# Gate and up projections with tokens standing and weight columns moving, in 29 groups of a two-layer kernel

## The chip, the cores and the metric

The kernel runs on one core of one Trainium2 chip. The metric is device time in microseconds of one execution; the number for a kernel is the median of several runs. A profiled execution, taken separately, gives the trace that all durations below come from.

## What is computed

Two layers of two blocks each, on x of 2048 tokens by 512 features in bf16, with the same weights in both layers:

```
x = x + A(layernorm(x), k, v, shift_k, ssm_k, ssm_D)
x = x + B(layernorm(x), w_gate, w_up, w_down)
(both once more)

A: kv = v * (k shifted over 4 taps with shift_k)
   y  = causal convolution of kv with ssm_k along the 2048 tokens, by FFT, + kv * ssm_D
   return layernorm(x) * y
B: return (silu(z @ w_gate) * (z @ w_up)) @ w_down      # w_gate, w_up: 512 x 1792; w_down: 1792 x 512
```

The convolution does not depend on x: k, v and the two filters are the same in both layers.

## The kernel before

The 2048 tokens are cut into four blocks c = 0..3 of 512, and each block into two halves h of two rows of 128 tokens (row o = 0, 1). A unit is (layer, c, h): 256 tokens in one layer; there are 16 units and they run in the order of c, then layer, then h. The convolution is done by matmuls with cosine and sine tables (tiles fwd and inv; X, G, H, Z are spectra), block against block, and its matrix products lie between those of the units, as do its elementwise products on DVE.

For a unit, `prologue` normalises the two rows, multiplies by y, adds, normalises again and writes z (128 tokens x 512 features) for each row. A transposing DMA from SP's queue turns z into zT, whose layout is [128 features, 4 feature blocks kd, row o, 128 tokens]. Only unit (0, 0, 0), the first, turns z on PE, and there ACT copies row 0 and DVE row 1 out of PSUM (lines 940 and 938).

`ffn(unit)` then walks the 14 blocks ft of 128 hidden columns in groups of 4, 4, 4 and 2. For each group `gate_up` makes gate and up, and `down` accumulates the group's share of the output in two PSUM tiles pd, one for each row. Six blocks (SHARE) are done for two units at once, with 512 moving columns. In `gate_up` the weights stand (128x128) and the 256 tokens of zT move, so the result comes out with hidden columns on partitions, which is the side on which `down` needs it as its standing operand:

```
mm(ps.t[:, q * m * W:(q + 1) * m * W],
   [(wt[which].t[:, kd, ft * P:(ft + 1) * P], moving(kd)) for kd in range(KD)])
```

Two blocks ft share one PSUM tile pf of 512 columns. ACT takes gate out of PSUM through silu into sg (line 974) and copies up into ht (line 977); DVE multiplies ht by sg (line 979). `down` (line 994) reads ht standing and w_down moving, 512 columns. Line 323 is the helper `mm` through which gate, up and most of the convolution go. At the end ACT copies pd (line 1075) and DVE adds it to x (line 1078).

All instructions are first recorded as operations with an engine, a cost, their readers and writers (class Plan). The order in which they are issued on every engine is a table, ORDER, written out in the file; `Plan.order` only places buffers in the slots of their rings along that order, and semaphores do the rest at run time. Each engine works its queue in this order. SP's queue holds all loads, stores and transposing DMAs. Rings have a number of slots each, among them n 2, sg 2, ht 5 (also for temporaries t1 and t2), dn 1, pf 4 (PSUM) and zT 3.

Of the kernel before, what the change touches and what calls it, by code (L numbers as in the profile page):

```python
# [53 lines left out]
SHARE = {(1, 0, 1): 2, (0, 2, 0): 2, (1, 3, 0): 2}  # L54
ORDER = [
# [59 lines left out]
NZ = 3  # L115
# [127 lines left out]
def kernel(  # L243
# [705 lines left out]
    def gate_up(us, fts, k):  # L949
        m, n = len(us), len(fts)  # L950
        per = 2 // m
        sg = new("sg", "sg", [P, n, m, W], parts=n // per)
        ht = new("ht", "ht", [P, n, m, W], parts=n // per)
        zs = [zts[u] for u in us]

# [385 lines left out]
```

## Time and profile before

| | |
|---|---|
| Median of 3 runs | 343.09 us (342.76 to 343.57) |
| Profiled execution | 342.9 us, of which the span of the trace 341.1 us |
| PE busy | 336.9 us, 2563 matmuls; clock granted 1.00 |
| DVE, ACT, POOL busy | 282.4, 252.5, 37.3 us |
| Matmuls of gate and up | 1696 with 256 columns, 48 with 512 |
| Matmuls of down | 434 with 512 columns, 28 in the last unit with 320 or 192 |
| Transposing DMAs of SBUF data | 30 of z, 16 of the convolution |
| q8, instruction fetches | 20 packets of 16 KB |

A busy time is the union of the instructions' spans on that engine. Matmuls are pipelined: the mean duration of one is longer than the distance from one to the next, and their ends are modelled. PEld is the weight load, which runs beside matmuls. In a group's line the number after x is the count, then come busy us and mean ns, then the idle time of the engine just before these instructions and what ended it. The chain of waits goes back from the last instruction, at each step to what released it, or to the instruction before it on its engine; its columns are start, length, engine, tile and line.

### The profile page before, as it was taken

To read this page: it belongs to the slowest core of one execution; us is meant where nothing else is said; L and a number is where in the kernel's file an instruction comes from. 1 tells how busy PE (TensorE), PEld (TensorE's weight loads), DVE (VectorE), ACT (ScalarE), POOL (GpSimd) and SP (SyncE) were. 2 spreads that over 40 slices of the span, in tenths; PEclk is the share of its full clock that TensorE was granted. 3 is DMA by queue.
4 is the path that set the end of the run, shared out by engine and by line. 5 is a ranking of instruction groups with operands and counts; after the bars stand their busy time and mean duration, and the time that the engine had idled before them with its cause. 6 is when DMAs were issued, how large, how long until landed. Compare 5 with 4: busy or idle time off the path is not lost.

```text
span 341.1 us, 6468 instructions
## 1 busy us (share of the span) xinstructions
PE 336.9 (99%) x2563; PEld 242.8 (71%) x2563; DVE 282.4 (83%) x478; ACT 252.5 (74%) x496; POOL 37.3 (11%) x46
## 2 busy tenths in 40 slices
PE   8999999999999999999999999999999999999996
PEld 7657858678687567768587756768685877777683
DVE  8899999999999999999999999889997533726022
ACT  7899999999977475778999973768665545545451
POOL 4000100002106100103100100101101000001000
PEclk9999999999999999999999999999999999999999
DMA  7999314050224175010110224010101110001111
GB/s 280 333 320 341 52 31 63 0 156 1 34 46 94 31 102 164 3 30 2 33 20 13 48 46 125 0 33 1 33 0 44 36 33 0 17 16 21 27 33 31
DMA packets 42088, 22.95 MB, mean 67 GB/s; under 512 B 33989, under 2 KB 39882, under 8 KB 42058
## 3 DMA queue, kind: packets, MB, share of 16 engines
q1 hardware_dynamic: 41904, 22.49, 26.0%
q8 instruction: 20, 0.33, 0.4%
q14 instruction: 10, 0.08, 0.1%
q10 hardware_dynamic: 154, 0.05, 0.1%
HBM read 12.33 MB, written 2.10 MB: 42 GB/s over the span
## 4 chain that ended last, share of the span: by engine, by line
PE 94%; ACT 3%; DMA 1%; SPq 0%; issue 0%; ACTq 0%
PE pf L323 57%; PE pd L994 28%; PE ps L323 6%; PE ps L470 2%; DMA kn<-in_A_k_dram 1%; ACT H L431 1%; ACT Yk L729 1%; ACT ks L526 0%; ACT n L874 0%; PE pt L378 0%; PE pt L489 0%; ACT zT L940 0%; ACT X L431 0%; SPq L354 0%; ACT xc L1052 0%
## 5 line engine op out<-in xcount | busy, mean ns | idle before, releaser
L323 PE MATMUL pf<-zT,wg_sb 128*128 128x256 bf16 (+1 forms) x872 | 110.3, 276 | 0.0
L323 PE MATMUL pf<-zT,wu_sb 128*128 128x256 bf16 (+1 forms) x872 | 110.0, 275 | 0.1
L994 PE MATMUL pd<-wd_sb,ht 128*128 128x512 bf16 (+1 forms) x462 | 106.2, 373 | 0.0
L323 PEld LDWEIGHTS <-wu_sb 128*128 128x128 bf16 x872 | 85.3, 98 | 18.9 <-issue 0.6
L323 PEld LDWEIGHTS <-wg_sb 128*128 128x128 bf16 x872 | 85.3, 98 | 17.3
L977 ACT CAST ht<-pf 128x512 bf16<-128x512 f32 x112 | 65.0, 592 | 23.0 <-PE pf L323 22.8
L974 ACT ACTIVATE sg<-pf 128x512 bf16<-128x512 f32 x112 | 66.6, 606 | 20.8 <-PE pf L323 17.3
L994 PEld LDWEIGHTS <-ht 128*128 128x128 bf16 x462 | 45.0, 98 | 44.1
L979 DVE TENSOR_TENSOR ht<-ht,sg 128x1024 bf16<-128x1024 bf16 (+1 forms) x61 | 38.9, 642 | 19.8 <-ACT ht L977 13.7
L826 POOL TENSOR_TENSOR rstd<-ve,nhalf 128x2 f32<-128x2 f32 x24 | 25.1, 1047 | 192.6 <-DVE ve L824 192.6
L821 DVE BATCH_NORM_STATS2 bnst<-xc 128x6 f32<-128x512 bf16 x48 | 31.8, 684 | 0.5
L1075 ACT CAST dn<-pd 128x512 bf16<-128x512 f32 x30 | 17.2, 590 | 17.5 <-PE pd L994 17.5
L431 ACT ACTIVATE X<-ps 128x512 bf16<-128x512 f32 x32 | 18.9, 606 | 10.5 <-PE ps L323 10.0
L1078 DVE TENSOR_TENSOR xc<-xc,dn 128x1024 bf16<-128x1024 bf16 x15 | 10.3, 687 | 16.8 <-ACT dn L1075 16.8
L669 DVE TENSOR_TENSOR t<-X,G 128x2048 bf16<-128x2048 bf16 x18 | 21.9, 1218 | 0.1
L665 DVE TENSOR_TENSOR t<-X,G 128x2048 bf16<-128x2048 bf16 x18 | 21.9, 1219 | 0.0
L855 POOL TENSOR_TENSOR rstd<-ve,nhalf 128x2 f32<-128x2 f32 x8 | 8.4, 1052 | 78.5 <-ACT ve L853 78.5
L679 DVE TENSOR_TENSOR Z<-Z,t 128x2048 bf16<-128x2048 bf16 x12 | 14.7, 1221 | 0.3
L677 DVE TENSOR_TENSOR t<-t,t 128x2048 bf16<-128x2048 bf16 x12 | 14.6, 1220 | 0.2
L431 ACT ACTIVATE H<-ps 128x512 bf16<-128x512 f32 x24 | 14.2, 612 | 0.0
L901 DVE TENSOR_TENSOR n<-n,Yk 128x1024 bf16<-128x1024 bf16 x15 | 10.3, 690 | 3.1 <-ACT n L874 1.9
L323 PE MATMUL ps<-hs,fwd 128*128 128x512 bf16 x40 | 12.7, 379 | 0.1
(103 smaller groups left out, 321.8 us busy)
## 6 DMA issues: line engine op xcount, KB each, us to landing
hn<-in_A_ssm_k_dram SPq DMA_DIRECT2D x4, 512.0 KB, 5.5
vt<-in_A_v_dram SPq DMA_DIRECT2D x4, 512.0 KB, 5.6
xc<-in_A_q_dram SPq DMA_DIRECT2D x4, 512.0 KB, 4.9
out_dram<-xc SPq DMA_DIRECT2D x15, 128.0 KB, 1.8
wg_sb<-in_B_w_gate_dram SPq DMA_DIRECT2D x1, 1792.0 KB
wu_sb<-in_B_w_up_dram SPq DMA_DIRECT2D x1, 1792.0 KB, 8.0
wd_sb<-in_B_w_down_dram SPq DMA_DIRECT2D x1, 1280.0 KB, 11.6
kn<-in_A_k_dram SPq DMA_DIRECT2D x1, 512.0 KB, 4.3
```

The source lines that it names most:

```text
L323: nc.tensor.matmul(o, lhsT=lhsT, rhs=rhs, start=(n == 0), stop=(n == len(terms) - 1))
L431: add("ACT", act(D), lambda: nc.scalar.activation(out=view(), in_=ps.t[:], func=ACT.Copy, scale=scale), r=[ps], w=[(buf, keys)], conv=conv)
L665: dve(n * D, lambda t1=t1, part=part: nc.vector.tensor_mul(out=t1.t[:], in0=x.t[:, sl, 0, :], in1=g.t[:, sl, part, :]), [(x, key(slots, (0 ...
L669: dve(n * D, lambda t2=t2, part=part: nc.vector.tensor_mul(out=t2.t[:], in0=x.t[:, sl, 1, :], in1=g.t[:, sl, 1 - part, :]), [(x, key(slots ...
L679: dve(n * D, lambda t1=t1, part=part: nc.vector.tensor_add(out=z.t[:, sl, part, :], in0=z.t[:, sl, part, :], in1=t1.t[:]), [t1], [zk], con ...
L821: add("DVE", 0.6, lambda st=st, i=i: nc.vector.bn_stats(out=st.t[:], in_=xs[c].t[:, i, :]), r=[(xs[c], (i,))], w=[st])
L826: add("POOL", pw, lambda: nc.gpsimd.tensor_tensor(out=rstd.t[:], in0=ve.t[:], in1=nhalf.t[:].to_broadcast((P, n)), op=ALU.pow), r=[ve, nha ...
L974: add("ACT", act(D), lambda ps=ps, sl=sl: nc.scalar.activation(out=sg.t[:, sl], in_=ps.t[:], func=ACT.Silu), r=[ps], w=[(sg, (b,))], due=( ...
L977: add("ACT", act(D), lambda ps=ps, sl=sl: nc.scalar.copy(out=ht.t[:, sl], in_=ps.t[:]), r=[ps], w=[(ht, (b,))], due=(us[0], at, 1.5, "a"))
L979: dve(n * m * W, lambda: nc.vector.tensor_mul(out=ht.t[:], in0=ht.t[:], in1=sg.t[:]), [sg], [ht], due=(us[0], (k + n) / NF, 0.0, "h"))
L994: nc.tensor.matmul((pds[o] if not cs.start else pds[HP]).t[:, cs], lhsT=ht.t[:, q, at, o * P:(o + 1) * P], rhs=wt["d"].t[:, ft, cs], start ...
L1075: add("ACT", act(D), lambda o=o: nc.scalar.copy(out=dn.t[:, o, :], in_=pds[o].t[:]), r=[pds[o]], w=[(dn, (o,))], due=(unit, 1.0, 3.0, "h"))
```

## The change

In 13 of the 16 units the first two or three groups of four blocks ft (WIDE) are made by a new function, with operands exchanged: 128 tokens of zT stand and 512 columns of the weights move. That gives the result with tokens on partitions, one PSUM tile per row o. The product of gate and up is therefore turned by two transposing DMAs on SP's queue into the layout that `down` reads; `down` for row o waits for the part of row o only.

```
+WIDE = {(1, 3, 1): 3, (0, 3, 1): 2, (0, 3, 0): 3, (1, 2, 0): 2, (0, 2, 1): 2, (1, 1, 0): 3, (0, 1, 0): 2, (1, 0, 0): 2, (0, 0, 0): 2, (1, 2, 1): 2, (1, 1, 1): 2, (0, 1, 1): 2, (0, 0, 1): 2}
 ORDER = [
...
-    plan = Plan({"h": 1, ... "t4": 2, "n": 2, "jk": 1, "dn": 1, "ks": 2, "z": 3, "zT": NZ,
-                 "sg": 2, "ht": 5, "st": 8, ...
+    plan = Plan({"h": 1, ... "t4": 2, "jk": 1, "ks": 2, "z": 3, "zT": NZ,
+                 "w2": 10, "st": 8, ...
...
+    def gate_up_wide(unit, fts, k):
+        zT, f0 = zts[unit], fts[0] * P
+        sg = new("w2", "sg", [P, HP, D], parts=HP)
+        hn_ = new("w2", "hw", [P, HP, D], parts=HP)
+        ht = new("w2", "ht", [P, KD, 1, W], parts=HP)
+        for o in range(HP):
+            for which in ("g", "u"):
+                ps = new("pf", "pf", [P, D], F32)
+                def go(ps=ps, o=o, which=which):
+                    mm(ps.t[:], [(zT.t[:, kd, o, :], wt[which].t[:, kd, f0:f0 + D]) for kd in range(KD)])
+                add("PE", pe(KD, D), go, r=[(zT, (o,)), wt[which]], w=[ps], ...)
+                if which == "g":
+                    add("ACT", act(D), lambda ps=ps, o=o: nc.scalar.activation(out=sg.t[:, o], in_=ps.t[:], func=ACT.Silu), ...)
+                else:
+                    add("ACT", act(D), lambda ps=ps, o=o: nc.scalar.copy(out=hn_.t[:, o], in_=ps.t[:]), ...)
+        dve(HP * D, lambda: nc.vector.tensor_mul(out=hn_.t[:], in0=hn_.t[:], in1=sg.t[:]), [sg], [hn_], ...)
+        for o in range(HP):
+            add("SP", 1.25, lambda o=o: nc.sync.dma_start_transpose(
+                out=ht.t[:, :, 0, o * P:(o + 1) * P], in_=hn_.t[:, o].rearrange("p (k f) -> p k f", k=KD)),
+                r=[(hn_, (o,))], w=[(ht, (o,))], lat=1.5)
+        return ht
...
-        groups = left + [(None, rest[a:min(a + 4, cut)], (unit,)) for a in range(0, cut, 4)] \
+        groups = left + [(None, rest[a:min(a + 4, cut)], (unit,) if a // 4 >= WIDE.get(unit, 0) else None) for a in range(0, cut, 4)] \
...
-                ht = gate_up(us, fts, k)
+                ht = gate_up(us, fts, k) if us else gate_up_wide(unit, fts, k)
```

The rings n, sg, ht and dn become one ring w2 of ten slots of the same size, used also by the new tile hw. The table ORDER is another one throughout, with entries for the new operations: what follows what on every engine is new, not only around the new groups. A third way to start the first spectrum is added that is not selected. The numbers of operations on ACT, DVE and POOL and their sizes stay; PE has 2097 matmuls instead of 2563 (464 fewer in the groups, 2 fewer that only keep PE busy at the start), and SP has 58 more transposing DMAs of 128 x 512 each.

More of the change, by code (lines that the diff above doesn't have):

```diff
@@ L289, in span @@
         return slice(rows[0], rows[-1] + 1, rows[1] - rows[0])
-    plan = Plan({"h": 1, "k": 1, "v": 1, "hs": 1, "x": 2, "y": 2, "s8": 10, "t4": 2, "n": 2, "jk": 1, "dn": 1, "ks": 2, "z": 3, "zT": NZ,
-                 "sg": 2, "ht": 5, "st": 8, "mv": 6, "ve": 6, "rs": 6, "pf": 4, "pc": 2, "pd": 2, **RINGS})
+    plan = Plan({"h": 1, "k": 1, "v": 1, "hs": 1, "x": 2, "y": 2, "s8": 10, "t4": 2, "jk": 1, "ks": 2, "z": 3, "zT": NZ,
+                 "w2": 10, "st": 8, "mv": 6, "ve": 6, "rs": 6, "pf": 4, "pc": 2, "pd": 2, **RINGS})
     def new(ring, name, shape, dtype=BF16, parts=1):
@@ L651, in product @@
             sl = slots[0]
-            t1, t2 = new("ht", "t1", [P, 2, D]), new("ht", "t2", [P, 2, D])
+            t1, t2 = new("w2", "t1", [P, 2, D]), new("w2", "t2", [P, 2, D])
             for t, part in ((t1, 0), (t2, 1)):
@@ L746, in pair_product @@
     def pair_product(a, b, dst, slot, ks):
-        t1, t2 = new("ht", "t1", [P, 2, D]), new("ht", "t2", [P, 2, D])
+        t1, t2 = new("w2", "t1", [P, 2, D]), new("w2", "t2", [P, 2, D])
         for t, part in ((t1, 0), (t2, 1)):
@@ L888, in apply_norm @@
         nmr = shift_of(st, HP, due) if on_act or N_ACT(layer, c, h) else None
-        n = new("n", "n", [P, HP, D], parts=HP)
+        n = new("w2", "n", [P, HP, D], parts=HP)
         for o, i in enumerate(rows):
@@ L951, in gate_up @@
         per = 2 // m
-        sg = new("sg", "sg", [P, n, m, W], parts=n // per)
-        ht = new("ht", "ht", [P, n, m, W], parts=n // per)
+        sg = new("w2", "sg", [P, n, m, W], parts=n // per)
+        ht = new("w2", "ht", [P, n, m, W], parts=n // per)
         zs = [zts[u] for u in us]
@@ L980, in gate_up @@
         return ht
+    def gate_up_wide(unit, fts, k):
+        zT, f0 = zts[unit], fts[0] * P
+        assert list(fts) == list(range(fts[0], fts[0] + KD))
+        sg = new("w2", "sg", [P, HP, D], parts=HP)
+        hn_ = new("w2", "hw", [P, HP, D], parts=HP)
+        ht = new("w2", "ht", [P, KD, 1, W], parts=HP)
+        for o in range(HP):
+            at = (k + 2 * o) / NF
+            for which in ("g", "u"):
+                ps = new("pf", "pf", [P, D], F32)
+                def go(ps=ps, o=o, which=which):
+                    mm(ps.t[:], [(zT.t[:, kd, o, :], wt[which].t[:, kd, f0:f0 + D]) for kd in range(KD)])
+                add("PE", pe(KD, D), go, r=[(zT, (o,)), wt[which]], w=[ps], due=(unit, at + (which == "u") / 21, 0.0, None))
+                if which == "g":
+                    add("ACT", act(D), lambda ps=ps, o=o: nc.scalar.activation(out=sg.t[:, o], in_=ps.t[:], func=ACT.Silu),
+                        r=[ps], w=[(sg, (o,))], due=(unit, at, 1.0, "a"))
+                else:
+                    add("ACT", act(D), lambda ps=ps, o=o: nc.scalar.copy(out=hn_.t[:, o], in_=ps.t[:]),
+                        r=[ps], w=[(hn_, (o,))], due=(unit, at, 1.5, "a"))
+        dve(HP * D, lambda: nc.vector.tensor_mul(out=hn_.t[:], in0=hn_.t[:], in1=sg.t[:]), [sg], [hn_], due=(unit, (k + KD) / NF, 0.0, "h"))
+        for o in range(HP):
[3 more added lines that the diff above has]
+        return ht
     def down(unit, pds, ht, fts, us, k, first, end, own):
@@ L990, in go @@
                 def go(o=o, css=css):
-                    at = sorted(zts[u].slot for u in us).index(zts[unit].slot)
+                    at = sorted(zts[u].slot for u in us).index(zts[unit].slot) if us else 0
                     for cs in css:
@@ L998, in down @@
                 add("PE", pe(n) if not last else pe(n, css[0].stop - css[0].start), go,
-                    r=[ht, (wt["d"], sorted({int(ft >= GROUPS[0]) for ft in fts}))],
+                    r=[(ht, (o,)) if us is None else ht, (wt["d"], sorted({int(ft >= GROUPS[0]) for ft in fts}))],
                     w=[pds[o]] if not split else [pds[o], pds[HP]] if not last else [pds[HP if css[0].start else o]],
@@ L1030, in ffn @@
             if ht is None:
-                ht = gate_up(us, fts, k)
-                if len(us) > 1:
+                ht = gate_up(us, fts, k) if us else gate_up_wide(unit, fts, k)
+                if us and len(us) > 1:
                     shared.setdefault(nxt, []).append((ht, fts, us))
@@ L1072, in ffn @@
             rows = rows_of(h)
-            dn = new("dn", "dn", [P, HP, D], parts=HP)
+            dn = new("w2", "dn", [P, HP, D], parts=HP)
             for o in range(HP):
@@ L1100 @@
     h0 = load_h(0, "ACT", -70) if HQ == "ACT" else None
-    tapR = new("dn", "tapR", [KD, P, KS])
+    tapR = new("w2", "tapR", [KD, P, KS])
     def load_taps(after=()):
@@ L1229 @@
             butterfly(evx, X[0], 0, False)
+        elif X0 == "mix":
+            evx = spectrum("evx")
+            X[0] = spectrum("X0")
+            direct(vt[0], X[0], "pf", eng(XVE[:4]), (0, 2))
         else:
@@ L1235 @@
             butterfly(ev, G[0], 1, False)
-        if X0 == "half":
+        if X0 in ("half", "mix"):
             half(vt[0], evx, "bd", 1.0, "pf", eng(XVE[4:]), False)
```

117 rows, old and new, of the table ORDER are left out of this document.

## The prediction

> **What bounds the kernel now.** I read the page first, then the chain of waits in order of time, then the timelines of PE, ACT and DVE around 32 us, the groups by form, the windows, and last the transfers' landing times.
>
> ```profile
> PE 336.9 (99%) x2563; PEld 242.8 (71%) x2563; DVE 282.4 (83%) x478; ACT 252.5 (74%) x496; POOL 37.3 (11%) x46
> ```
>
> ```profile
> 31.57 0.62 ACT zT L940
> 32.23 1.91 PE pf L323 x16
> ...
> 284.99 10.48 PE pf L323 x96
> 295.47 6.04 PE pd L994 x28
> ...
> 332.49 5.66 PE pd L994 x38
> 338.17 0.32 ACT xc L1052
> ```
>
> From 32.23 to 338.17 us the chain holds nothing but PE. The view of waits gives PE two in all, 0.8 and 0.2 us, both before 6 us. The chain also gives what a matmul costs when others follow it: 10.48 us / 96 = 109.17 ns with 256 moving columns, 6.04 / 28 = 215.71 ns with 512. The means in the groups (273 and 379 ns) are latencies and overlap, so I don't use them.
>
> ```profile
> 31.28 0.42 DVE L938 COPY zT<-ptz 128x512 bf16<-128x512 bf16 x1
> 31.57 0.62 ACT L940 COPY zT<-ptz 128x512 bf16<-128x512 bf16 x1
> 32.23 1.91 PE L323 MATMUL pf<-zT,wu_sb 128*128 128x256 bf16 x16
> ```
>
> The first gate/up matmul waits for both halves of the first zT: DVE's copy is done at 31.70, ACT's at 32.19.
>
> ```profile
> L974 ACT ACTIVATE sg<-pf 128x512 bf16<-128x512 f32 x112 | 66.6, 606 | 20.8 <-PE pf L323 17.3 <-DVE ht L979 2.8
> L977 ACT CAST ht<-pf 128x512 bf16<-128x512 f32 x112 | 65.0, 592 | 23.0 <-PE pf L323 22.8
> L979 DVE TENSOR_TENSOR ht<-ht,sg 128x1024 bf16<-128x1024 bf16 x51 | 34.8, 685 | 19.3 <-ACT ht L977 13.5 <-ACT sg L974 5.7
> ```
>
> ```profile
> 30.00:60.00 30.00, 29.82 (x243) 22.74 (x241) 29.83 (x44) 29.71 (x66) 3.21 (x4) 1.00 0.43 84
> 60.00:90.00 30.00, 30.00 (x216) 20.94 (x215) 29.56 (x55) 29.65 (x60) 3.81 (x5) 1.00 0.22 54
> ...
> 270.00:300.00 30.00, 30.00 (x226) 21.95 (x225) 12.61 (x26) 14.95 (x28) 1.38 (x2) 1.00 0.12 27
> ```
>
> Columns: window, length, then busy time of PE, PEld, DVE, ACT, POOL, granted clock, DMA share, GB/s. Until 90 us all three engines are full; from 270 on DVE and ACT are half idle. The clock is 1.00 throughout.
>
> ```profile
> L908 SPq DMA_TRANSPOSE zT<-z x30: 1189/1210/2272, 47.6 to 314.1; - x30
> ...
> DMA to landing us min/median/max: 2.4/2.5/4.2
> ```
>
> This is the row for the transfer that the change adds: one 128x512 transpose holds SP's queue for 1.2 us and lands 2.4 to 4.2 us after its issue.
>
> **Part 1, matmuls.** The WIDE values add up to 29 groups. Such a group had 32 matmuls of 256 columns (4 column blocks x 4 terms x gate and up) and gets 16 of 512: the same 8192 columns, 16 instructions fewer. 32 x 109.17 = 3.493 us against 16 x 215.71 = 3.451 us. Over 29 groups: 464 x (2 x 109.17 - 215.71) = 464 x 2.63 ns = **1.22 us less**, all of it on the chain. The 512-column price also holds with a gate/up tile as output: the shared groups of before run eight of them from 201.38 to 203.11 us in PE's timeline, 216 ns each. The weight loads (98 ns each, 464 fewer, 45 us of PEld) lie beside matmuls and give nothing. A rule of the Trainium skill (Perfetto Trace Analysis, Identifying the Most-Contended Engine) would have me judge PE's headroom by LDWEIGHTS busy time and not by matmul busy time: by it PE has 29% of the span free and the 45 us would look like a prize. The spacing of 109 and 216 ns speaks against that here.
>
> **Part 2, the start.** In the new order PE's first 8 wide matmuls read only the second half of zT, the one DVE copies; only the ninth waits for ACT. So the start can move from 32.23 to DVE's 31.70 plus a hop, about 31.75: 0.48 us. ACT's zT copy now stands behind a squared-sum pass (0.62 us with its read) and an X eviction (0.48): 31.57 + 1.10 + 0.62 = 33.29, needed at 31.75 + 8 x 0.2157 = 33.48. Covered, with 0.2 to spare; if that cover fails, the loss is the same order as the gain. Against it: ACT does one H eviction more (0.48) ahead of the first Yk, on which the chain to zT hangs. Bounds: 0.5 gained to 0.3 lost; I take **0.25 gained**, the middle of what remains when the H eviction is half hidden.
>
> **Part 3, evictions and products.** Per group four ACT evictions of 512 columns and one DVE product of 1024, before and after, on the same shapes: no change in busy time. Nothing else on ACT, DVE or POOL is added; the rest of the order table only moves work.
>
> **Part 4, the transposes.** 58 new SP transposes, 58 x 1.21 = 70 us of SP's queue, which otherwise mostly waits. They lengthen the way from a group's last gate/up matmul to its first down matmul: 0.6 (eviction) + 0.7 (product) before, now + 2.5 = 3.8 us for the first half and 1.2 more for the second. What hides that is PE work placed between the two. I counted it in the new order, each matmul at the prices above: of 29 groups 17 have over 8 us, five have 7.0 to 7.8 and seven have 5.6 to 6.5 (the least is in the last unit); the second half's down has 7.3 us or more. So every group has at least 1.8 us over the bare chain. What can eat this is queueing ahead of the evictions and products: in the trace of before the product was ready 1.1 to 8.9 us after the last matmul, mostly 2 to 4, and the tightest group still had 0.3 us left. With 2 to 4 plus 2.5 the seven tight groups come out between +1 and -0.5 us, the others positive.
>
> A second eater is a late landing. Seven of the 46 transposes of SBUF data in before took 3.2 to 4.2 us, and during each an instruction fetch ran (queue q8, 20 packets of 16 KB, about 1.1 us each, or q14). With 104 such transposes some nine of the new ones meet one and are 0.2 to 1.8 us late; most have that slack. I allow **0.2 us** of waits (bounds: none, and 2 us if three or four tight groups are hit).
>
> Loads in the same queue: the wide transposes right behind a load are those after hn and kT of block 2 (cover 10.4), after x of block 2 (10.2), after kT of block 3 (8.2), between the halves at v of block 3 (17.4), and after x of block 3 (7.4). An x load lands 3.3 us after its issue at 208.30 in before. The Trainium skill (DMA: Bandwidth & Descriptors, Queues, rings and completion order) says that each DMA engine takes a ring's descriptors in order, so a transpose would wait out all of such a load; no run here shows a transpose behind an x load. By the rows, 3.8 + 3.3 = 7.1 us against 7.4: it just fits.
>
> Buffers: n, sg, ht, t1, t2 and dn had 2 + 2 + 5 + 1 = 10 slots in four rings and share 10 now. A wide group holds three (sg, hw, ht) where a narrow one holds two; the row of before shows a wait of this kind, 2.8 us of ACT on ht L979, which PE never felt.
>
> The tail (338.17 to 341.1) ends in the same last narrow group and the same two stores: no change.
>
> **Sum.** The profiled execution took 342.9 us (span 341.1 and 1.8 around it), 0.2 under the median of 343.09. 342.9 - 1.22 - 0.25 + 0.2 = 341.6; against the median of runs **341.8 us**.
>
> **Rivals.**
> (a) The waits eat the gain: one to two us of PE waits for late ht halves, in the seven tight groups. For: their slack is within the spread of the queueing seen before. Against: before ran with 0.3 to 1 us of slack in many groups without one wait. Time: 341.8 + 0.6 to 2.0 = 342.4 to 343.8.
> (b) Slower: the full stage from 32 to 92 us. DVE and ACT are 99% busy there, and in it two products of before were ready only 5.2 to 5.4 us after their last matmul. A wide group adds 2.5 for the first half: 7.8 us against covers of 7.4 to 8.9 in five of its six groups. The rival decides from a lag above about 5 us; each us beyond is then PE idle, and with DVE full there it isn't made up, since the later convolution blocks hang on DVE. Six groups at 0.5 to 1 us: 341.8 + 3 to 6 = 344.8 to 347.8; half of them, 343.8 to 345. Against: PE of the same stage shows no wait at all now, and this order was laid out with longer covers.
> (c) The change saves nothing per matmul: the 512 form with weights moving runs slower than 215.7, say 218 ns. Then 1.22 is gone and the time is 343.0. The shared groups speak against it; their moving operand is zT, not the weights, which is all that is left of this.
> (d) More is gained than these terms: the start moves further, or weight loads do hold PE back and 464 fewer of them help. 341.0 or less. For: nothing but the 0.5 us at the start; against: the matmul spacing, which bounds the second at nothing.
>
> **How the numbers follow.** No change within 0.2% (about what a measurement of this kernel can tell) is 342.40 to 343.78. The forecast, 341.2 to 342.4: 0.58. (d): 0.04. (a) 0.15 and (c) 0.03, both inside the band: 0.18. (b): 0.20. Faster 0.62, same 0.18, slower 0.20. The range runs from 341.1, the sum with the whole 0.5 us of the start and no wait, to 344.4, which takes in (a), (c) and the milder half of (b); about 0.15 is left out. The forecast's own range is 341.2 to 342.4.
>
> **What would show it.** Right: PE's matmul count 2097, 464 of them 128x512 with wg_sb or wu_sb moving, at 215 to 216 ns; the chain all PE from about 31.8 to 336.5 us; PE's waits on ht still near zero. Wrong: lines of PE pd waiting for an ht transpose in the view of waits. At 300 us these would be (a), at 40 to 90 us (b); DMA to landing of ht with a median well over 2.5 would show the transfer itself mispriced.

## The result, and the profile after

The changed kernel takes 345.86 us in the median of six runs (345.02 to 346.91); the kernel before, on the same chip, 343.19 us (342.76 to 343.57). The ratio is 1.0078, 95% interval 1.0059 to 1.0098: **slower by 2.7 us**, where 1.3 us faster was forecast. The profiled execution took 345.6 us, its span 343.8, at a granted clock of 1.00.

The first part of the forecast is there. The page's engine line has 2097 matmuls, and the chain of waits (start, length, engine, tile, line) has long stretches of wide ones at the forecast price: 13.81 us / 64 = 215.8 ns. The transposes land 2.5 us after their issue in the median, the last line below (from the page's DMA issues).

```profile
PE 337.6 (98%) x2097; PEld 197.6 (57%) x2097; DVE 281.3 (82%) x478; ACT 251.9 (73%) x496; POOL 41.3 (12%) x46
```

```profile
318.36 13.81 PE pf L327 x64
```

```profile
ht<-hw SPq DMA_TRANSPOSE x58, 2.5
```

What is new is in the window from 30 to 60 us. Columns as in the prediction: window, length, busy time of PE, PEld, DVE, ACT, POOL, clock, DMA.

```profile
30.00:60.00 30.00, 27.70 (x171) 15.33 (x169) 26.94 (x44) 26.25 (x58) 5.40 (x3) 1.00 0.46 98
```

Before, PE, DVE and ACT had 29.82, 29.83 and 29.71 us of work in this window. Now all three stand still in it for 2.3 to 3.8 us. Only POOL has more to show, 5.40 us instead of 3.21, with three operations instead of four. An engine that does less and takes longer is the place to look. The chain of waits of that stretch names it:

```profile
38.30 0.30 ACT ve L857
...
38.67 4.03 POOL rstd L859
...
42.72 0.48 ACT nmr L871 x2
43.20 0.48 ACT sg L1001
...
46.10 1.91 PE pf L327 x16
```

The operation is tiny: `rstd`, a power of a 128x2 tile, for the second norm of unit (0, 0, 1). It reads `ve`, the variance with epsilon added, which ACT makes. The shortest of its kind in the same trace take 0.69 us, and 12 of the 32 take over 1.2. This one is the longest: 4.03 us in the chain, 4.01 in POOL's timeline. Behind it on ACT stands `nmr`, a scale that needs it, and behind `nmr`, in the same queue, the evictions sg and hw of the wide groups, which do not. ACT is idle for 3.17 us; two PSUM tiles stay full; PE has no tile to write to:

```profile
PE pf L327 <- ACT sg L1001: 1.9, 1, 1.9
```

That is the only long wait in PE's view of waits, and it is not for an ht transpose. DVE's timeline shows what went on beside the rstd:

```profile
37.45 0.69 DVE L825 BATCH_NORM_STATS2 bnst<-xc 128x6 f32<-128x512 bf16 x1
38.05 1.21 DVE L597 TENSOR_TENSOR G<-H,G 128x2048 bf16<-128x2048 bf16 x1
39.18 0.68 DVE L1006 TENSOR_TENSOR hw<-hw,sg 128x1024 bf16<-128x1024 bf16 x1
39.78 1.22 DVE L597 TENSOR_TENSOR G<-H,G 128x2048 bf16<-128x2048 bf16 x1
40.92 1.22 DVE L673 TENSOR_TENSOR t<-X,G 128x2048 bf16<-128x2048 bf16 x1
44.88 0.69 DVE L1006 TENSOR_TENSOR hw<-hw,sg 128x1024 bf16<-128x1024 bf16 x1 [2.75 <-ACT hw L1004]
```

Four operations on two bf16 tiles each follow each other without a gap. (All of DVE's elementwise operations on two bf16 tiles are called products here; the two on G are a sum and a difference.) The rstd starts inside the first and ends at 42.68, 0.55 us after the last: the rstd was not done until DVE had run dry, and DVE ran dry only because its next product needed what ACT could not evict.

The ledger of PE, all from its timelines (a wait is the distance from one matmul's start to the next, less the price of a matmul, so 2.05 where the view of waits has 1.9): the first FFN matmul comes at 32.58 instead of 32.23 (+0.35); waits of 2.05, 0.31 and 0.33 us between 43 and 47 us (+2.69) and of 0.77 us in all elsewhere, the longest 0.30 at 153 us; the matmuls 1.22 less. 0.35 + 2.69 + 0.77 - 1.22 = 2.6 us. The last matmul ends 2.7 us later than before, and the tail behind it is as it was.

### The profile page after: what moved, and what is told of

It is laid out like the page before. It is cut to its first block, busy times and chain, and to the rows that moved or that the text cites. A ratio compares the mean times of both kernels' runs of the same rounds, so it can differ in the third digit from the quotient of the medians.

```text
span 343.8 us, 5684 instructions
## 1 busy us (share of the span) xinstructions
PE 337.6 (98%) x2097; PEld 197.6 (57%) x2097; DVE 281.3 (82%) x478; ACT 251.9 (73%) x496; POOL 41.3 (12%) x46
## 4 chain that ended last, share of the span: by engine, by line
PE 88%; ACT 8%; POOL 1%; DMA 1%; issue 0%; DVE 0%; ACTq 0%
PE pf L327 54%; PE pd L1025 27%; PE ps L327 6%; POOL rstd L859 1%; DMA zT<-z 1%; ACT H L435 1%; ACT X L435 1%; PE wm L1342 1%; ACT n L878 1%; ACT jk L849 1%; PE pt L493 1%; ACT hs L503 1%; ACT ks L530 0%; ACT Yk L733 0%; ACT sg L1001 0%; ACT hw L1004 0%
## 5 line engine op out<-in xcount | busy, mean ns | idle before, releaser
L327 PEld LDWEIGHTS <-zT 128*128 128x128 bf16 x464 | 45.2, 98 | 52.6 <-DMA zT<-z 0.6
L327 PE MATMUL pf<-wg_sb,zT 128*128 128x512 bf16 x232 | 57.4, 379 | 0.1
L327 PE MATMUL pf<-wu_sb,zT 128*128 128x512 bf16 x232 | 56.8, 379 | 0.0
L327 PE MATMUL pf<-zT,wu_sb 128*128 128x256 bf16 (+1 forms) x408 | 54.0, 279 | 2.2 <-ACT sg L1001 1.9
L327 PE MATMUL pf<-zT,wg_sb 128*128 128x256 bf16 (+1 forms) x408 | 53.8, 279 | 0.0
L327 PEld LDWEIGHTS <-wu_sb 128*128 128x128 bf16 x408 | 39.8, 98 | 15.2 <-issue 3.0
L327 PEld LDWEIGHTS <-wg_sb 128*128 128x128 bf16 x408 | 39.9, 98 | 11.4
L1004 ACT CAST hw<-pf 128x512 bf16<-128x512 f32 x58 | 33.7, 593 | 14.8 <-PE pf L327 14.4
L981 ACT CAST ht<-pf 128x512 bf16<-128x512 f32 x54 | 31.1, 592 | 10.8 <-PE pf L327 10.5
L1006 DVE TENSOR_TENSOR hw<-hw,sg 128x1024 bf16<-128x1024 bf16 x29 | 19.9, 688 | 22.3 <-ACT sg L1001 13.6
```

What stands on the lines that cost most here:

```text
L327: nc.tensor.matmul(o, lhsT=lhsT, rhs=rhs, start=(n == 0), stop=(n == len(terms) - 1))
L981: add("ACT", act(D), lambda ps=ps, sl=sl: nc.scalar.copy(out=ht.t[:, sl], in_=ps.t[:]), r=[ps], w=[(ht, (b,))], due=(us[0], at, 1.5, "a"))
L1004: add("ACT", act(D), lambda ps=ps, o=o: nc.scalar.copy(out=hn_.t[:, o], in_=ps.t[:]), r=[ps], w=[(hn_, (o,))], due=(unit, at, 1.5, "a"))
L1006: dve(HP * D, lambda: nc.vector.tensor_mul(out=hn_.t[:], in0=hn_.t[:], in1=sg.t[:]), [sg], [hn_], due=(unit, (k + KD) / NF, 0.0, "h"))
```

## The experiments

The theories, as the expectations name them. **P**: DVE's back-to-back products keep POOL's rstd off; what waits is ACT's queue behind nmr, and through it PE. **W**, the rival, is (b) of the prediction: the wide groups' longer way (eviction, product, transpose) is too long for the full stage, and the rstd is only the first to show it. Later ones (P1 to P3, T) are stated where they are used. Where a queue was reordered, the diff shows the engine's queue, not the table ORDER.

**1. Move what waits (act_later).** ACT's queue, everything else unchanged:

```
 sg<-pf (L1001), hw<-pf (L1004)
-nmr x2, sg<-pf, n, hw<-pf, n, sg<-pf x2 (L978)
+sg<-pf, hw<-pf, sg<-pf x2 (L978), nmr x2, n x2
```

> The changed kernel; on ACT alone four instructions (two nmr and the two normalise passes n that read POOL's rstd of about 38.7 us) stand behind three more evictions of gate and up. Theory P (DVE's tensor products keep POOL off, ACT's queue waits for POOL, PE for ACT's evictions): POOL's rstd may still take 3 to 5 us, but PE's waits of 2.7 us between 41 and 46 us go: 343.2 to 343.7 us. Theory W (the wide groups' longer way loads the full stage before 92 us): nothing changes, 345.5 to 346.3.

Measured: 344.42 us (343.65 to 346.25), ratio to before 1.0033 (1.0014 to 1.0052). The rstd is as long as before, 4.62 us, and ends again 0.55 us after DVE's last product. But the evictions no longer stand behind it, and PE's wait for sg is gone; 0.9 us for an X eviction and 1.1 us in three waits for ht remain. The time is 0.7 us above the upper end expected, and the gain is half of the 2.7 us. The X eviction of the 0.9 us still stands behind nmr and n in ACT's queue, from 45.48 us. So at least half of the damage is done by what is queued behind nmr.

**2. Let POOL in (bnst_between).** One BN_STATS of DVE, which had stood ahead of the four products, goes behind the first:

```
-BN_STATS bnst<-xc
 TENSOR_TENSOR G<-H,G
+BN_STATS bnst<-xc
 TENSOR_TENSOR hw<-hw,sg
 TENSOR_TENSOR G<-H,G
 TENSOR_TENSOR t<-X,G
```

> The changed kernel; on DVE alone one BN_STATS instruction (0.6 us, the same work) stands behind the first of the two G products at 38 us instead of ahead of it, so that it follows POOL's start. Theory P: POOL's rstd there takes 0.7 to 1.3 us instead of 4.0, ACT waits under 0.3 us for it, PE's 2.7 us of waits go: 343.1 to 343.6 us. Theory W: 345.5 to 346.3, whatever POOL does.

Measured: 342.44 us (341.91 to 343.79), ratio 0.9978 (0.9964 to 0.9993). POOL's timeline, then DVE's:

```profile
38.41 0.69 POOL L859 TENSOR_TENSOR rstd<-ve,nhalf 128x2 f32<-128x2 f32 x1 [7.70 <-ACT ve L857]
```

```profile
37.33 1.22 DVE L597 TENSOR_TENSOR G<-H,G 128x2048 bf16<-128x2048 bf16 x1
38.47 0.69 DVE L825 BATCH_NORM_STATS2 bnst<-xc 128x6 f32<-128x512 bf16 x1
39.07 0.67 DVE L1006 TENSOR_TENSOR hw<-hw,sg 128x1024 bf16<-128x1024 bf16 x1
```

The rstd is done in 0.69 us, beside the BN_STATS, and the time is below the range expected. The chain of waits from 36 to 50 us is PE alone, as in before. The wide groups, the transposes and every other order are those of the changed kernel; so W falls as the cause of the 2.7 us.

**3. The same order with narrow groups (narrow_same, narrow_bnst).** `WIDE = {}`, the transposes' entries taken out of the order, the rest as in the changed kernel and as in bnst_between.

> The changed kernel's order on PE, ACT, DVE, POOL and SP, but all 29 wide groups made the narrow way again (weights standing, 256 columns, no transposes of hw). Theory P: the wait sits in the order, so ACT still waits over 1.5 us for POOL near 40 us; with 1.2 us more of matmuls and a first unit that needs ACT's zT copy (up to 1.2 us later) 346.5 to 348.5. Theory W: without wide groups the waits go, 343.0 to 344.5 plus what the start costs.

> The same narrow groups in the same order, with the BN_STATS moved as in bnst_between. Theory P: 1.2 us (464 x 2.6 ns of matmul) plus 0 to 1.2 us at the start over bnst_between, so 344.4 to 346.0, and 1.5 to 3 us under narrow_same. Theory W: equal to narrow_same within 0.5 us, and below bnst_between.

Measured: 356.12 us (1.0365, 1.0333 to 1.0397) and 355.47 us (1.0356, 1.0329 to 1.0383). Both theories missed by far. PE waits 9.0 us in eight places for zT in the first and 8.3 in seven in the second: a narrow matmul needs both rows of zT, a wide one only its own, and this order issues the first matmuls of a unit when one row is there. POOL's rstd comes 2.7 us later than in the changed kernel in the first and 0.7 us later in the second, and takes 0.69 us in both, so the stall isn't there to be compared. The two say nothing on P or W. An order belongs to its operations; taking the operations back out of it is no clean undo.

**4. Take the matmuls' gain away (split_cols).** bnst_between, with

```
-mm(ps.t[:], [... wt[which].t[:, kd, f0:f0 + D] ...])
+for n in range(0, D, W):
+    mm(ps.t[:, n:n + W], [... wt[which].t[:, kd, f0 + n:f0 + n + W] ...])
```

> The kernel with the BN_STATS between the products (bnst_between), but each of the 464 wide matmuls of 512 moving columns is issued as two of 256 columns into the two halves of the same bank; tokens still stand, the order of every engine is otherwise the same. Theory P (the wide matmuls gain what the forecast's first term said, 464 x 2.63 ns, and POOL's held-off rstd took more than that back): 1.2 us above bnst_between, so 343.4 to 343.9, ratio to before 1.000 to 1.002; the split matmuls at 109.2 ns. Theory W (the wide matmuls gain nothing that reaches the end, because the wide groups' longer way sets the pace): within 0.3 us of bnst_between's 342.4.

Measured: 345.12 us (344.5 to 346.61), ratio 1.0046 (1.0027 to 1.0064). It lost 1.7 to 2.3 us against the two measurements of bnst_between (0.9978 above, 0.9997 below), more than the 1.2 expected; by the intervals it may be anything from 0.7 to 3.2 us. In its chain the split matmuls run at 8.73 us / 80 = 109.1 ns, so 1.22 us of it is the term itself. The rest is not settled; the page shows 20 instruction fetches instead of 16, and PE's timeline a wait of 0.85 us at 317 us. That the matmuls of the wide form gain 1.2 us is shown by their spacing, and that a gain reaches the end by the time; its size there is not told to better than a microsecond.

**5. Lengthen the transposes (turn_twice).** bnst_between, with a second transpose, of three of the four blocks, into a spare tile ahead of each of the 58:

```
+nc.sync.dma_start_transpose(out=spare[:], in_=hn_.t[:, o, P:].rearrange(...))
 nc.sync.dma_start_transpose(out=ht.t[:, :, 0, o * P:(o + 1) * P], in_=...)
```

> bnst_between with each of the 58 new ht transposes preceded by a second one of three of its four blocks into a spare tile that nobody reads (58 more SP commands of some 1.2 us; the output is the same). Each ht half then lands about 1.2 to 2.4 us later. Theory P (the transposes are hidden under 5.6 us and more of cover, except where they meet an instruction fetch): 0.3 to 1.5 us above bnst_between, 342.7 to 344.0, PE waits on ht only in a few places. Theory W (the wide groups' way through SP and the DMA is what sets the pace): 3 us or more above it, over 345.5, with PE waits on ht in most of the 29 groups.

Measured: 391.09 us (1.1357, 1.1305 to 1.1409), 48 us more. PE's view of waits:

```profile
PE pd L1029 <- DMA ht<-hw: 33.1, 25, 3.3
```

By the expectation's terms this is W: over 345.5 us, with waits in most groups. But the push is larger than meant. I had priced the delay at 1.2 to 2.4 us a half. All dummies write one tile and wait for each other (SP's view of waits has eight such waits, 4.5 us in all), so the second half of the first group is issued at 45.19 instead of 41.01 us, 4.2 later. The granted clock is lower too, 0.964 to 0.982 over the six runs, and how much of the 48 us that makes is open. So the run doesn't show that the transposes set the pace in the changed kernel, where PE's view has no wait for one. It still corrects my picture: in bnst_between the time from a half's landing to the first matmul that reads it is 2.2 us in the median (quartiles about 1.2 and 4.0), under 1 us for about ten of 58, and 0.05 us or less for three, of which PE waited for two. The transposes are covered, but not deeply.

**6. Mend the next wait (hw_earlier).** In bnst_between PE's longest wait of the FFN is

```profile
PE pd L1025 <- DMA ht<-hw: 1.4, 2, 1.2
```

It is for a transpose issued at 83.22 that landed 4.21 us later. Its product is moved ahead on DVE:

```
 n<-xc x2 (L883)
+hw<-hw,sg (L1006)
 Z<-m (L562), n<-n,Yk (L905)
-hw<-hw,sg (L1006)
```

> bnst_between, and one more DVE step moved: the second hw product of the group at 82.47 us goes ahead of the Z and n*Yk products (81.26 to 82.47), so that its two transposes are issued 1.2 us earlier. In bnst_between PE waits 1.2 us at 87.4 for the last of them, which met an instruction fetch and landed 4.2 us after its issue. Theory P (what is left of losses are single late steps, each with its own cause): that wait goes, 341.2 to 341.9, ratio 0.994 to 0.997. Theory W (the wide groups as a whole are too late, and the wait comes up at the next one): 342.2 to 342.7.

Measured: 343.08 us (342.46 to 345.25), ratio 0.9988 (0.9966 to 1.001). The wait at 87 us is gone and one of 0.79 us stands at 89.5, for a narrow group's DVE product. Expected 0.994 to 0.997, so a miss: in this profile a smaller wait stands at the next group, and no gain over bnst_between can be told. Nor can the missing wait at 87 us be put down to the move alone, as experiment 9 shows.

**7. The same trap without wide groups (before_rstd_late).** The kernel before, all groups narrow; on ACT

```
 ht<-pf (L977)
-ve (L853)
 ht<-pf (L977), sg<-pf x2 (L974)
+ve (L853)
 nmr x2
```

> The kernel before, all groups narrow, with one ACT step moved: ve of the second on_act norm (36.59 us) goes behind the two sg that follow it, so POOL's rstd starts at about 38.7 instead of 37.0, as in the changed kernel, beside the products t, t, n*Yk that DVE runs back to back. Theory P (it is DVE's products behind POOL's start, not the wide groups): rstd lasts 2.5 to 4.5 us instead of 1.5, PE waits 1 to 3 us between 40 and 47, and the time is 344.3 to 346.3, ratio 1.003 to 1.009. Theory W (only wide groups are short of slack here): rstd 1.5 us or less, or longer with no PE wait; 343.0 to 343.8. A rstd of 1.5 us with a loss under 1 us would leave open what lets POOL in.

Measured: 349.05 us (347.61 to 350.64), ratio 1.0153 (1.0115 to 1.0191). POOL's timeline, then PE's, then the windows:

```profile
38.84 3.44 POOL L855 TENSOR_TENSOR rstd<-ve,nhalf 128x2 f32<-128x2 f32 x1 [8.33 <-ACT ve L853]
```

```profile
43.33 1.87 PE L323 MATMUL pf<-zT,wu_sb 128*128 128x256 bf16 x8 [2.28 <-ACT sg L974]
```

```profile
40.00:43.00 3.00, 1.05 (x10) 0.79 (x9) 1.74 (x2) 0.69 (x3) 2.28 (x1) 1.00 0.00 0
43.30:46.60 3.30, 3.26 (x15) 2.15 (x15) 1.85 (x3) 3.30 (x7) 0.00 (x0) 0.50 0.00 0
```

The trap is the same in a kernel without a wide group: rstd 3.44 us, PE's wait for sg 2.28. So it is not a property of the wide form but of when ACT's ve falls among DVE's products. The time is 2.7 us above the upper end expected (the profiled run, 347.65 us, 1.3 above it). Part of that is the clock: after 2.4 us in which PE started no matmul the granted clock is 0.50 for 3.4 us, and the matmuls in it come about 105 ns later each, 1.6 us in all. All six runs of this kernel have a mean clock of 0.995.

**8. What lets POOL in (tiny_copy, tiny_product, bnst_again).** The changed kernel, with one DVE instruction of 128x2 floats ahead of the first hw product (and a memset of its tile at the start). P1: the kind of the instruction decides; P2: its length; P3: any break in the row of long products will do.

```
 TENSOR_TENSOR G<-H,G
+tiny_copy:    nc.vector.tensor_copy(out=tiny[:, 2:4], in_=tiny[:, 0:2])
+tiny_product: nc.vector.tensor_mul(out=tiny[:, 2:4], in0=tiny[:, 0:2], in1=tiny[:, 0:2])
 TENSOR_TENSOR hw<-hw,sg
```

> The changed kernel with one instruction more: a DVE copy of a 128x2 float tile that nobody reads, between the first G product and the first hw product (39.2 us), where bnst_between had put a BN_STATS. Everything else is the changed kernel's order. Theory P1 (POOL gets in at a DVE instruction that reads one tile, however short): rstd ends at once behind it, 0.7 to 1.5 us instead of 4.0, the PE waits of 2.7 us at 43 to 47 go, 342.4 to 343.4. Theory P2 (POOL gets in only while DVE does something else for as long as the rstd takes): rstd stays at 3 to 4 us, 345.0 to 346.5. Theory W (wide groups' longer way): as P2.

> As tiny_copy, but the instruction put between is a product of two 128x2 float tiles, so an instruction that reads two tiles, like its neighbours, but short and of another type. Theory P1 (the kind decides: one tile read lets POOL in, two do not): rstd stays at about 4 us and the time at 345.0 to 346.5. Theory P3 (any short gap or change of mode between the long bf16 products lets POOL in): rstd 0.7 to 1.5 us and 342.4 to 343.4. Theory W: 345.0 to 346.5.

> bnst_between once more, on the same chip as tiny_copy. Every theory: 342.2 to 342.8 in the median, ratio to before 0.997 to 0.999; by theory P tiny_copy differs from it by less than 0.6 us, by theory W by more than 2.

Measured: tiny_copy 342.78 us (342.18 to 343.8), ratio 0.998 (0.9963 to 0.9997); tiny_product 342.96 us (342.06 to 346.34), 0.9999 (0.9974 to 1.0024); bnst_again 343.61 us (342.14 to 345.1), 0.9997 (0.9974 to 1.002). POOL and DVE of tiny_copy:

```profile
39.14 1.17 POOL L859 TENSOR_TENSOR rstd<-ve,nhalf 128x2 f32<-128x2 f32 x1 [7.70 <-ACT ve L857]
```

```profile
39.66 0.17 DVE L1012 COPY tiny<-tiny 128x2 f32<-128x2 f32 x1
39.75 0.68 DVE L1014 TENSOR_TENSOR hw<-hw,sg 128x1024 bf16<-128x1024 bf16 x1
```

An instruction of 0.17 us that computes nothing of use takes the changed kernel from 1.0078 to 0.998. The product does the same as the copy, so P1 and P2 fall and P3 stands:

```profile
38.45 1.16 POOL L859 TENSOR_TENSOR rstd<-ve,nhalf 128x2 f32<-128x2 f32 x1 [7.72 <-ACT ve L857]
```

Nor is it the moment of the rstd's start: it starts 0.60 and 0.62 us into the G product in these two, and 0.62 and 0.61 us into it in the changed kernel and act_later, where it takes 4.01 and 4.62. bnst_again came out 1.2 us above bnst_between, against an expectation of 342.2 to 342.8: a second measurement of one kernel, on another chip, moves by more than the differences between these repaired ones, and I rank none of them.

**9. A second place (two_tiny).** tiny_copy, with one more copy where the rstd had taken 3.06 us at 77.5 us, and with the move of hw_earlier.

> tiny_copy, with a second such copy between the m product and the hw product at 78.7 us, where POOL's rstd took 3.06 us in three kernels, and with the hw product of hw_earlier moved. So the transposes that PE waits for at 87 us are issued some 1.2 us earlier, and the second long rstd goes too. Theory P: rstd 0.7 to 1.8 us at both places, no PE wait over 0.3 us at 87 to 90, 341.8 to 342.7 in the median, ratio to before 0.995 to 0.998. Theory T (what is left is the thin cover of the ht transposes in many groups, and one wait removed is met again at a later group): PE waits on ht of 0.5 us and more elsewhere, 342.4 to 343.3.

Measured: 342.93 us (342.67 to 344.21), ratio 0.9986 (0.9969 to 1.0003). POOL's timeline of bnst_between and then of this kernel, and the second copy on DVE:

```profile
77.52 3.06 POOL L830 TENSOR_TENSOR rstd<-ve,nhalf 128x2 f32<-128x2 f32 x1 [0.94 <-DVE ve L828]
```

```profile
77.57 0.72 POOL L830 TENSOR_TENSOR rstd<-ve,nhalf 128x2 f32<-128x2 f32 x1 [0.94 <-DVE ve L828]
```

```profile
78.79 0.16 DVE L1012 COPY tiny<-tiny 128x2 f32<-128x2 f32 x1
```

The short rstd is not the copy's work: it ended at 78.29 us, before the copy began. bnst_again, the same kernel as bnst_between and without a copy, has a short one here as well:

```profile
77.20 0.72 POOL L830 TENSOR_TENSOR rstd<-ve,nhalf 128x2 f32<-128x2 f32 x1 [0.94 <-DVE ve L828]
```

So at this place the rstd is let in or kept off from one execution to the next, and the experiment says nothing on what a copy does here. It matters, though. In bnst_between, tiny_copy and tiny_product the rstd takes 3.06 us here, DVE stands 0.59 us for it, and PE waits 0.9 to 1.2 us at 87 to 88 us for a transpose; in bnst_again and split_cols it takes 0.72 and 0.71 and no such wait stands there. These are single profiles, but they suggest that the wait of experiment 6 hangs on the same trap as well as on the late landing. The end doesn't move in two_tiny: PE meets 0.69 us at 89.8 us for a DVE product. By its expectation's terms T has this one.

## Why the prediction was wrong

**Part 1 was right.** 464 x 2.63 ns = 1.22 us less; the wide matmuls run at 215.8 ns, split in two they run at 109.1, and the split kernel loses 1.7 to 2.3 us. (c) falls, and PEld as a measure of headroom with it (the rule of the Trainium skill, Perfetto Trace Analysis, Identifying the Most-Contended Engine, that the prediction set aside): PEld fell from 242.8 to 197.6 us and nothing came of it.

**Part 2 had the sign wrong here.** The half start exists: the first wide matmul starts 0.05 us after DVE's copy ends, while ACT's copy ends 1.2 us later still. But the chain to z is later by more than it gives: ACT's first Yk is at 26.74 us instead of 26.04, and DVE's zT copy ends at 32.53 instead of 31.70. Against 0.25 gained, 0.35 lost. The six repaired kernels, with the same start, began between 31.91 and 33.06 us, so about nothing is the fair price, and a single profile doesn't tell it to better than half a microsecond.

**Part 3 is the step that failed**: "Nothing else on ACT, DVE or POOL is added; the rest of the order table only moves work." I priced the moves at nothing because busy times stay. What the order moved was ACT's ve, from 36.59 to 38.30 us, and with it POOL's rstd, from 37.02 (1.49 us long, let in between two G products) to 38.67, under another row of products where it was not let in. That cost 2.7 us. The rows that gave the warning are in the trace of before, and no row of POOL's timeline enters the prediction: an rstd of 1.49 us at this very place, one of 0.69, and one of 6.21.

```profile
37.02 1.49 POOL L855 TENSOR_TENSOR rstd<-ve,nhalf 128x2 f32<-128x2 f32 x1 [6.87 <-ACT ve L853]
45.45 0.69 POOL L826 TENSOR_TENSOR rstd<-ve,nhalf 128x2 f32<-128x2 f32 x1 [6.93 <-DVE ve L824]
```

```profile
105.56 6.21 POOL L826 TENSOR_TENSOR rstd<-ve,nhalf 128x2 f32<-128x2 f32 x1 [11.57 <-DVE ve L824]
```

The last cost nothing there: PE's view of waits in before has no wait after 6 us. The Trainium skill (SBUF — State Buffer, SBUF: two separate sides) has a rule that goes with these rows: VectorE and GpSimd share a pair of ports, which is locked and not divided; when a VectorE instruction with two SBUF inputs meets a GpSimd one that reads SBUF, whichever starts first has the pair for its whole instruction, and the other stands still. The traces agree with POOL's standing still, 0.69 against 4.01 and 6.21 us; they add that POOL can lose at several ends of products in a row, which the length of one instruction (1.2 us) would not give. That the ports are the cause is not shown by any run here.

**Part 4 was right in kind and too small in size.** The transposes cost 1.2 us of SP and land after 2.5 us; eight of the 43 whose landing the trace gives took over 3 us in the changed kernel. The row that the prediction lacked is there too: a transpose of hs issued at 135.96 us, 0.4 behind an x load, landed 3.8 us later, 0.5 after the load. PE's gaps ahead of down matmuls were 0.4 us there, against 0.2 allowed. With the big stall repaired the view of waits has 1.4 us in bnst_between and 1.1 in tiny_copy, but 0.4 in bnst_again. In bnst_again's profile the forecast's other terms nearly come out: the first FFN matmul starts 0.2 us earlier than before, and the execution takes 342.1 us, where the sum said 341.6. The repaired kernels' runs, at 0.9978 to 0.9999, gain 0 to 0.8 us and not 1.3; waits for halves and the start can make up the difference, but no run separates them.

**The rivals.** (b) had the sign, the stage (32 to 92 us) and its reason, that nothing can be made up where ACT and DVE are full. Its mechanism was another: not a late ht half but a late eviction, behind an operation of another engine. That 345.86 lies within its 344.8 to 347.8 is luck. (a) is part of what is left after the repair. (d) did not happen.

**The sums.** Three of the prediction's numbers don't follow from its own terms; none of them changes the account. The sum with the whole 0.5 us of the start and no wait is 341.35, not 341.1. Three groups of (b) at 0.5 to 1 us come to 343.3 to 344.8, not 343.8 to 345. Covers of 5.6 to 6.5 us less 4.5 to 6.5 leave +2.0 to -0.9, not +1 to -0.5.

## What to carry to other kernels

A new order of a full kernel is not free because the busy times are the same: for every operation that one engine hands to another, look up its longest row in the trace of before, not its mean, and ask who is queued behind its reader. A small operation on POOL beside back-to-back two-input products on DVE is such a one. Put its reader behind the evictions, which brought half of the loss back here, or break DVE's row with a short instruction right after the operation is released, which at 38 us brought all of it back, with each of three instructions. And one profile of such a kernel is not enough: the same operation can be let in in one execution and kept off in the next. When a stage suddenly has all busy engines idle, look for the one whose busy time grew while its count did not.

## What the hardware showed that I had not expected

- POOL's 128x2 rstd ends a fixed time after a DVE product. In the traces of before and after there are 17 that took over 1.2 us; every one ends 0.547 to 0.553 us after the end of a bf16 product. How many such ends it misses first varies from none to six, also where DVE goes from one product straight to the next; what decides it is not settled. At 38 us a BN_STATS or an instruction of 0.17 us between two products was enough in every profile that had one; at 77 us one kernel without a break shows 3.06 us in one profile and 0.72 in another.
- A gap of 2.4 us in PE's work was followed by 3.4 us at a granted clock of 0.50 in before_rstd_late; the one of 2.05 us in the changed kernel's profile was not. The length alone does not decide: gaps of 3.1 us at 130 to 132 us were followed by it in narrow_same and not in narrow_bnst.
- A transpose of 128x512 that lands 2.5 us after its issue in the median took 4.2 us where it met an instruction fetch (83.22 us in bnst_between).
